# One planner attribute for the "own term" copies, and a new order of all engines, in an RWKV-6 + channel-MLP kernel

## The chip, the cores and the metric

The kernel runs on one core of a Trainium2 chip. The metric is the device time of the whole launch in microseconds, as a median over runs; lower is better.

## What is computed

An RWKV-6 attention block feeds a channel MLP with a residual. Everything is float32; B = 4, H = 8, S = 768, D = 48, so the model width is H*D = 384.

```python
# attention: r, k, v, w (B, H, S, D), u (H, D)
for t in range(S):
    cur = einsum('bhd,bhe->bhde', u[None] * k[:, :, t], v[:, :, t])
    y[:, :, t] = einsum('bhd,bhde->bhe', r[:, :, t], state + cur)
    state = w[:, :, t, :, None] * state + einsum('bhd,bhe->bhde', k[:, :, t], v[:, :, t])
x = y.transpose(0, 2, 1, 3).reshape(B, S, H * D)
# MLP
xn = (x - mean) / sqrt(var + 1e-6) * g_ln
out = x + maximum(xn @ w_ch1, 0) @ w_ch2        # w_ch1 (384, 1536), w_ch2 (1536, 384)
```

## The kernel before

**Tiling.** The work is cut into eight rounds (4 batches x 2 halves of 384 steps). A round has three tiles of 128 steps; each tile is cut into chunks of 64 steps, and a chunk into groups of four steps (Q = 4). Round 0 is done in two parts, its first tile alone (part c0 = 0) and its other two tiles (c0 = 1), so that the first products can start early.

**Front of a round.** `load` fetches w, k and r (`nat_w`, `nat_k`, `nat_r`). `inner` forms the products inside a group of four steps (`pad_k`, `pad_r`, `rk`, and again `nat_k`, `nat_r`, `nat_w`), and reductions write the sums to `vals`. These sums, the "own terms" (a step with itself and with the steps of its own group), go to DRAM (`own_d`) and come back in another layout as `va`. `place_own` then copies them into the diagonal of the matrix `A` with a predicated copy: data `va`, mask `mask_own`, both in SBUF. There are 18 such copies, all on DVE. `turn` transposes `pad_k` and `pad_r` on PE (`k_ps`, `r_ps`) and ACT copies them out; `turn_w` does the same for the decays (`w_ps`). For four levels, `quads` multiplies r by k on PE in many small matmuls (`a<-r,k`), `grow` scales k and r on DVE by the decays `tot` (`k<-k,tot`), and `keep` copies a level's result from PSUM into `A` (DVE: `A<-mask,a`). `states` makes and scans the states (`a<-v,k` on PE, `s<-s,decay,a` on DVE). `inside` multiplies `A` by v (`a<-v,A`, `a<-vx,A`), `outputs` adds the states' part (`a<-s,r`).

**Back of a round.** `normalize` (`stats`, `mv`, `rstd`, `xn`), transposes (`xT_ps`), and the MLP. Round 0 multiplies by the weights directly (`h_ps<-xf,w`); from round 1 on, x and the weights are cut in high, low and difference parts (`xhl`, `xd`; `wh`, `wl`, `w1diff`), and a round's first product starts with `h_ps<-xd,d`. `convert` turns the loaded weights into floats (`raw`, `held`, `w<-w`, `w<-w,held`, `ffn`).

**What sets the order.** Each step is handed to `Plan.add` with its engine (or a choice of engines), a cost, what it reads and writes, and the buffers that it takes. A table, `ORDER`, then lists every step once: the entry modulo 10000 is the step, the thousands choose among the engines that it may run on. `Plan.order` walks through that table, keeps a clock for each engine by the costs, and from it decides three things: which home (SBUF slot or PSUM bank) a buffer gets, how many filler matmuls (`idle`) go in front of a PE step that is planned to wait for more than 0.35 us, and which DVE steps a GpSimd step has to wait for. Each engine then runs its steps in the order of the table.

**The shared port.** `Plan.add` takes `port`, true for steps that may run on GpSimd and for those that say so. Such steps are planned one after the other on DVE and GpSimd:

```python
if op.port and e in held:
    t = max(t, held["POOL" if e == "DVE" else "DVE"])
...
if op.port and e in held:
    held[e] = t + cost
```

A filler is put in only where a PSUM bank of kind `b` is free by the plan at that time:

```python
home = min(self.homes[idle[0]], default=None)
if n and home and home[0] <= free["PE"]:
    out.append(lambda n=n, home=home: idle[2](n, home[1]))
```

## Time and profile before

| | before |
|---|---|
| median of 3 runs | 469.9 us (469.14 to 469.95) |
| span of the profiled execution, first to last instruction | 466.7 us |
| median less span | 3.2 us |
| PE busy | 458.0 us (98% of the span), 7442 records |
| DVE busy | 353.2 us (76%), 742 instructions |
| ACT busy | 263.8 us (57%), 608 instructions |
| GpSimd (POOL) busy | 137.7 us (30%), 141 instructions |

The execution that was profiled has no time of its own beside its span; a time is worked out here as a change of that span, set against the median. All instructions go through one helper, so they carry one line (L47) and are told apart by the names of their tiles, `out<-in`. A busy PE is not a PE that does useful work: fillers count as busy, and the ends of matmuls are modelled. Each float32 matmul of the fillers and of the small products leaves two records in the trace.

### The profile page before, as it was taken

Reading aid. Unit: us, or ns where it says so; the run is one execution under the profiler, and the core shown is the slowest. Engines: PE = TensorE matmul, PEld = TensorE weight load, DVE = VectorE, ACT = ScalarE, POOL = GpSimd, SP = SyncE. Lnnn points to the kernel's source line nnn. Section 1 sums busy time; section 2 is a strip of 40 time slices with the busy share of each in tenths; the row PEclk is TensorE's granted clock in tenths of the full one; section 3 lists DMA queues with packets and bytes.
Section 4 is the critical chain, followed back from the end, with each engine's and each line's share of the span. In section 5 each row is a group of like instructions: output and inputs, shape, how many; then the busy total and the mean of one; then the engine's idle time right before and its main releaser. Section 6 shows DMA issues by size and latency. Waiting matters only on the chain.

```text
span 466.7 us, 17460 instructions
## 1 busy us (share of the span) xinstructions
PE 458.0 (98%) x7442; PEld 399.7 (86%) x7442; DVE 353.2 (76%) x742; ACT 263.8 (57%) x608; POOL 137.7 (30%) x141
## 2 busy tenths in 40 slices
PE   8999999999999999999999999999999999999996
PEld 5677989766999666989776899999999999999996
DVE  8999999999997768897879887976733535525535
ACT  4697889754765322665621677855555456444440
POOL 4137013332451242353443240221013122321030
PEclk9999999999999999999999999999999999999999
DMA  7987775776658505745630545302222232142011
GB/s 208 277 199 210 205 156 137 233 196 156 174 150 185 111 28 136 166 138 145 157 61 5 86 124 129 111 30 70 84 62 67 76 103 67 37 136 67 35 51 51
DMA packets 105501, 56.23 MB, mean 120 GB/s; under 512 B 61904, under 2 KB 102352, under 8 KB 105424
## 3 DMA queue, kind: packets, MB, share of 16 engines
q1 hardware_dynamic: 105152, 54.92, 45.1%
q8 instruction: 58, 0.95, 0.9%
q10 hardware_dynamic: 272, 0.20, 0.1%
q14 instruction: 19, 0.16, 0.1%
HBM read 45.27 MB, written 7.47 MB: 113 GB/s over the span
## 4 chain that ended last, share of the span: by engine, by line
PE 84%; DVE 10%; POOL 2%; issue 2%; SPq 1%; DMA 1%; DVEq 0%; POOLq 0%
PE h_ps L47 28%; PE a L47 26%; PE o L47 15%; PE o_2P L47 4%; PE o_2D L47 2%; PE k_ps L47 2%; PE r_ps L47 2%; PE kn_ps L47 2%; PE xT_ps L47 2%; DVE nat_k L47 1%; DVE s L47 1%; DVE A L47 1%; SPq L47 1%; DVE vals L47 1%; DMA nat_k<-in_k_dram 1%
## 5 line engine op out<-in xcount | busy, mean ns | idle before, releaser
L47 ACT ACTIVATE h<-h_ps 128x384 f32<-128x384 f32 (+2 forms) x108 | 47.8, 456 | 49.6 <-PE h_ps L47 48.9
L47 PE MATMUL o<-ffn,h 128*128 128x384 f32 x216 | 74.7, 492 | 0.0
L47 DVE SCALAR_TENSOR_TENSOR hD<-hH,hL 128x384 fp32r<-128x384 f32 x60 | 36.3, 616 | 37.1 <-POOL hL L47 16.0
L47 POOL TENSOR_TENSOR hL<-h,hH 128x384 fp32r<-128x384 f32 x28 | 30.1, 1081 | 102.7 <-PE a L47 27.7
L47 ACT ACTIVATE h_ps<-h_ps 128x384 f32<-128x384 f32 x84 | 39.7, 481 | 34.5 <-PE h_ps L47 33.5
L47 PEld LDWEIGHTS o<-ffn,h 128*128 128x128 f32 x216 | 39.2, 190 | 23.1
L47 PEld LDWEIGHTS a<-r,k 48*56 48x56 f32 (+3 forms) x3072 | 39.7, 122 | 10.5 <-issue 4.9
L47 PE MATMUL h_ps<-xd,d 128*128 128x384 f32 x204 | 47.1, 335 | 0.0
L47 PE MATMUL a<-r,k 48*56 48x32 f32 (+3 forms) x3072 | 44.1, 208 | 0.6 <-issue 0.2
L47 PE MATMUL h_ps<-xhl,wl 128*128 128x384 f32 x180 | 40.4, 334 | 0.0
L47 DVE TENSOR_TENSOR r<-r,tot 112x768 f32<-112x768 f32 (+1 forms) x40 | 32.2, 808 | 10.0 <-PE a L47 10.0
L47 PE MATMUL h_ps<-xhl,wh 128*128 128x384 f32 x180 | 39.1, 326 | 0.0
L47 ACT ACTIVATE hH<-h 128x384 fp32r<-128x384 f32 x60 | 29.7, 518 | 11.6 <-PE a L47 7.8
L47 DVE TENSOR_TENSOR k<-k,tot 112x768 f32<-112x768 f32 (+1 forms) x40 | 31.6, 790 | 5.5 <-PE a L47 5.4
L47 PEld LDWEIGHTS h_ps<-xd,d 128*128 128x128 f32 x204 | 34.0, 189 | 0.5
L47 DVE TENSOR_TENSOR hL<-h,hH 128x384 fp32r<-128x384 f32 x32 | 17.9, 568 | 20.0 <-PE a L47 9.5
L47 PEld LDWEIGHTS h_ps<-xhl,wh 128*128 128x128 f32 x180 | 30.8, 189 | 0.0
L47 ACT COPY A<-a 32x384 f32<-32x384 f32 (+5 forms) x56 | 23.5, 421 | 12.4 <-PE a L47 9.8
L47 PEld LDWEIGHTS h_ps<-xhl,wl 128*128 128x128 f32 x180 | 30.1, 189 | 0.2
L47 PE MATMUL a<-w2D,hD 128*128 128x384 f32 x90 | 29.7, 330 | 0.4 <-DVE hD L47 0.4
L47 PE MATMUL idle<-nought 128*128 128x384 f32 (+2 forms) x90 | 27.9, 431 | 0.9 <-DVE eps L47 0.9
L47 ACT ACTIVATE xf<-xT_ps,g_sb 128x384 f32<-128x384 f32 (+2 forms) x27 | 14.7, 549 | 22.1 <-PE xT_ps L47 18.9
(184 smaller groups left out, 1135.3 us busy)
## 6 DMA issues: line engine op xcount, KB each, us to landing
d<-w1d SPq DMA_DIRECT2D x84, 192.0 KB, 2.6
raw<-in_moe_w_ch_dram SPq DMA_DIRECT2D x24, 384.0 KB, 4.0
nat_r<-in_r_dram SPq DMA_DIRECT2D x24, 192.0 KB, 3.8
nat_w<-in_w_dram SPq DMA_DIRECT2D x24, 192.0 KB, 4.1
v<-in_v_dram SPq DMA_DIRECT2D x24, 192.0 KB, 4.2
nat_k<-in_k_dram SPq DMA_DIRECT2D x23, 192.0 KB, 3.9
out_dram<-x SPq DMA_DIRECT2D x15, 192.0 KB, 2.0
w1d<-w1diff SPq DMA_DIRECT2D x12, 192.0 KB, 2.9
```

The source lines that it names most:

```text
L47: ins = self.tc.keep_in_program_order(f(*args, **kw))
```

## The change

`place_own` hands its copies to the planner with `port=True`; before, these copies had no such mark, so that GpSimd's steps could be planned beside them. The mark itself gives no instruction. The table `ORDER` is another one: the steps stand in the order of their planned start times, and the order on every engine is new, as is the choice of engine for some steps. Fillers, homes of buffers and the DVE steps that GpSimd waits for follow from it. No step is added or taken away.

```diff
@@ class Plan @@
     ORDER = [
-        10008, 3, 4, 10012, 2, 9, 10, 5, 11, 16, 264, 261, 7, 14, 13, 18, 10019, 262, 17, 265, 260, 263,
...
+        2, 3, 4, 5, 260, 262, 263, 261, 12, 10, 14, 265, 9, 13, 8, 15, 264, 16, 25, 11, 110, 17, 65, 18, 26,
...
     ]
@@ place_own @@
             plan.add(
                 "DVE", cost(part, 0.155, 0.98), lambda j=j: place(j),
                 r=[(va, i, c0) for i in ((0,), (1, 2))[j]] + [(A_, "nought")] + after,
-                w=[(A_, 0, c0, j)], pri=urgent(part, 10),
+                w=[(A_, 0, c0, j)], pri=urgent(part, 10), port=True,
             )
```

In all, the program before has 45 filler matmuls on PE with 12,288 columns, the changed one 34 with 9,344; all of them stand ahead of PE's first products `h_ps<-xf,w`. Some steps change engines: among them four products `nat_k<-nat_k,nat_r` of a whole round leave GpSimd, which keeps none, for DVE; three squarings `nat_w<-nat_w` go the other way; ACT takes over both clearings of `A` and four more copies `x<-a`.

Three places are shown.

First DVE, up to the second pair of own-term copies of round 0 (part c0 = 1; `mask_own`). Before:

```order
L47 TENSOR_TENSOR nat_k<-nat_k,u_bc 128x1152
L47 COPY_PREDICATED A_83<-mask_own,va_374 128x4x64
L47 COPY s_647<-a_67 112x48 x2
L47 SCALAR_TENSOR_TENSOR s_647<-s_647,decay_201,a_67 112x48 x2
L47 COPY s_668<-a_66 112x48 x2
L47 SCALAR_TENSOR_TENSOR s_668<-s_668,decay_201,a_66 112x48 x2
L47 TENSOR_REDUCE vals_75<-nat_k 128x3x2x4
L47 COPY_PREDICATED A_83<-mask_own,va_374 128x2x4x64
L47 TENSOR_REDUCE vals_75<-nat_r 128x6x2x2
L47 COPY_PREDICATED A_83<-mask_own,va_374 128x2x4x64
L47 SCALAR_TENSOR_TENSOR s_647<-s_647,decay_201,a_67 112x48 x6
L47 SCALAR_TENSOR_TENSOR last_767<-s_647,decay_201,a_67 112x48 x2
```

And DVE at the same place now:

```order
L47 TENSOR_REDUCE vals_75<-nat_k 128x3x2x4
L47 BN_STATS stats_705<-x_667 128x6
L47 TENSOR_REDUCE vals_75<-rk_0_565 128x3x2x2
L47 BN_AGGR mv_706<-stats_705 128x2
L47 SCALAR_TENSOR_TENSOR s_585<-s_585,decay_176,a_67 112x48 x6
L47 SCALAR_TENSOR_TENSOR last_732<-s_585,decay_176,a_67 112x48 x2
L47 SCALAR_TENSOR_TENSOR s_607<-s_607,decay_176,a_66 112x48 x6
L47 SCALAR_TENSOR_TENSOR last_753<-s_607,decay_176,a_66 112x48 x2
L47 TENSOR_REDUCE vals_75<-nat_r 128x6x2x2
L47 COPY_PREDICATED A_83<-mask_own,va_302 128x2x4x64 x2
L47 TENSOR_SCALAR w_3_1_114<-w_3_1_114 128x384
L47 TENSOR_SCALAR w_3_2_115<-w_3_2_115 128x384
```

The pair of copies now stands together, behind the sixteen scan steps (`s`, `last`) and the first `stats`, which stood behind it before. Up to and with the second copy of the pair, DVE runs 93 instructions before and 107 now.

Then PE between the second `inside` of round 0 (`a<-v,A`, c0 = 1) and the first products, `h_ps<-xf,w`. Before, behind that `inside`:

```order
L47 MATMUL idle<-nought 128x128
L47 MATMUL a_67<-s_668,r_210 64x48 x16
L47 MATMUL r_ps_2_879<-ident,pad_r 112x128 x4
L47 MATMUL idle<-nought 128x128
L47 MATMUL xT_ps_2_0_898<-ident,xn_0_891 128x128
L47 MATMUL w_ps_0_903<-ident,w_73 112x128 x3
L47 MATMUL k_ps_1_907<-ident,pad_k 112x128 x4
L47 MATMUL xT_ps_0_0_919<-ident,xn_0_891 128x128
L47 MATMUL xT_ps_1_0_921<-ident,xn_0_891 128x128
L47 MATMUL a_66<-s_647,r_210 64x48 x16
L47 MATMUL idle<-nought 128x128
L47 MATMUL a_67<-r_802,k_872 60x32 x48
```

And now, ahead of that `inside` (it begins right behind the last row; no filler stands after it, and the first products follow on its `a<-s,r` and `w_ps`):

```order
L47 MATMUL xT_ps_0_0_750<-ident,xn_0_741 128x128
L47 MATMUL idle<-nought 128x384
L47 MATMUL k_ps_0_767<-ident,pad_k 112x128 x4
L47 MATMUL xT_ps_2_0_776<-ident,xn_0_741 128x128
L47 MATMUL k_ps_2_780<-ident,pad_k 112x128 x4
L47 MATMUL k_ps_1_786<-ident,pad_k 112x128 x4
L47 MATMUL r_ps_0_795<-ident,pad_r 112x128 x4
L47 MATMUL r_ps_2_803<-ident,pad_r 112x128 x4
L47 MATMUL r_ps_1_809<-ident,pad_r 112x128 x4
L47 MATMUL xT_ps_1_0_817<-ident,xn_0_741 128x128
```

All transposes of round 1 (`k_ps`, `r_ps`) and of the first normalized tile (`xT_ps`) have moved ahead of `inside`, and the three fillers behind it are gone; one product `a<-r,k` of 48 matmuls that stood ahead of the first products now stands behind nine of them.

Last the start of PE. Before:

```order
L47 MATMUL idle<-nought 128x384 x7
L47 MATMUL idle<-nought 128x128
L47 MATMUL k_ps_0_182<-ident,pad_k 112x128 x4
L47 MATMUL idle<-nought 128x384
L47 MATMUL idle<-nought 128x128
L47 MATMUL r_ps_0_191<-ident,pad_r 112x128 x4
L47 MATMUL w_ps_0_196<-ident,w_73 112x128
```

And now:

```order
L47 MATMUL idle<-nought 128x384 x3
L47 MATMUL idle<-nought 128x128
L47 MATMUL w_ps_0_166<-ident,w_73 112x128
L47 MATMUL idle<-nought 128x384 x3
L47 MATMUL idle<-nought 128x256
L47 MATMUL r_ps_0_190<-ident,pad_r 112x128 x4
L47 MATMUL idle<-nought 128x128
L47 MATMUL k_ps_0_203<-ident,pad_k 112x128 x4
```

The small transpose `w_ps` comes first, in the middle of the long stretch of fillers, and the fillers between the transposes are fewer.

## The prediction

> **What bounds the kernel now.** I read the page first: its busy line and the line of the chain.

> ```profile
> span 466.7 us, 17460 instructions
> PE 458.0 (98%) x7442; PEld 399.7 (86%) x7442; DVE 353.2 (76%) x742; ACT 263.8 (57%) x608; POOL 137.7 (30%) x141
> ...
> PE 84%; DVE 10%; POOL 2%; issue 2%; SPq 1%; DMA 1%; DVEq 0%; POOLq 0%
> ```

> PE is busy for 98% of the span, so a new order can win only what PE does for nothing: waits, and fillers, which count as busy. Next the view by windows, to see in which stage which engine is full (columns: length, then busy us and records of PE, weight loads, DVE, ACT, POOL; granted clock; DMA share; GB/s).

> ```profile
> 0.00:20.00 20.00, 17.48 (x155) 11.56 (x157) 18.16 (x44) 11.37 (x21) 5.99 (x18) 1.00 0.82 239
> 20.00:40.00 20.00, 19.76 (x444) 14.07 (x437) 19.85 (x49) 16.27 (x42) 9.86 (x8) 1.00 0.85 205
> 40.00:60.00 20.00, 19.36 (x549) 17.66 (x551) 19.21 (x50) 17.37 (x48) 6.20 (x8) 1.00 0.67 198
> 60.00:140.00 80.00, 80.00 (x1502) 64.83 (x1495) 78.00 (x161) 56.90 (x134) 27.25 (x24) 1.00 0.68 175
> 140.00:310.00 170.00, 169.01 (x3886) 140.19 (x3885) 140.07 (x295) 87.11 (x196) 55.26 (x54) 1.00 0.46 110
> 310.00:460.00 150.00, 150.00 (x930) 149.24 (x929) 74.42 (x142) 74.80 (x169) 33.19 (x31) 1.00 0.23 68
> ```

> From 310 us on PE is full and DVE half empty: nothing to win there. From 140 to 310 PE lacks 1.0 us, and DVE has 30 us to spare. Up to 140 us both look full, and DVE lacks only 4.8 us in all. The first stretch is where PE's fullness is false. The groups by line and form show the fillers (busy time, mean ns of one record; every filler leaves two):

> ```profile
> L47 PE MATMUL idle<-nought 128*128 128x384 f32 x44 | 18.7, 543 | 0.9 <-DVE eps L47 0.9
> L47 PE MATMUL idle<-nought 128*128 128x128 f32 x32 | 6.6, 287 | 0.0
> L47 PE MATMUL idle<-nought 128*128 128x256 f32 x14 | 4.6, 409 | 0.0
> ```

> That makes 22, 16 and 7 fillers, 29.9 us by these rows (a little less in truth, since neighbours overlap): six per cent of the kernel in which PE waits for the front of round 0. It waits there mainly for DVE, which runs 57.2 of the first 60 us. So two bounds follow each other: DVE until the first products can run freely, then PE. A gain must come from the first 50 us, and must survive until DVE has room at 140 us.

> **Part one, the fillers.** The changed program has 17, 12 and 5 fillers. At 18.7/22 = 0.85, 6.6/16 = 0.41 and 4.6/7 = 0.66 us each that is 14.5 + 4.9 + 3.3 = 22.7 us, 7.2 less than 29.9. But a filler only pictures a planned wait. Where no PSUM bank is free by the plan, none is put in, and PE simply waits. So -7.2 us is the favourable end of this term; the other end is 0, if every removed filler becomes a bare wait.

> **Part two, what DVE allows.** The second `inside` of round 0 needs the second pair of own-term copies. The timeline of DVE there:

> ```profile
> 38.48 1.13 DVE L47 COPY_PREDICATED A<-mask_own,va 128x512 f32<-128x512 int8 x1
> 39.50 1.34 DVE L47 TENSOR_REDUCE vals<-nat_r 128x24 f32<-128x1152 f32 x1
> 40.76 0.76 DVE L47 COPY_PREDICATED A<-mask_own,va 128x512 f32<-128x512 int8 x1
> 41.38 1.14 DVE L47 SCALAR_TENSOR_TENSOR s<-s,decay,a 112x48 f32<-112x48 f32 x6
> 42.42 0.45 DVE L47 SCALAR_TENSOR_TENSOR last<-s,decay,a 112x48 f32<-112x48 f32 x2
> ```

> The pair ends at 40.76 + 0.76 = 41.52. In the new order sixteen scan steps come first: (42.42 - 41.38)/6 = 0.173 each, +2.8 us. Of the other steps that cross this point two more leave than enter (107 against 93 instructions up to here, sixteen of them the scan). Their sizes run from 0.76 to 1.34 us by the neighbours above; I take the two at the lower end of that, -1.5 in all, with 0 and -2.7 as bounds. Two copies of one size took 1.13 and 0.76: the longer one had GpSimd work beside it, and the new plan keeps such steps apart, -0.4 (bounds 0 and -0.4). The pair then ends at 41.52 + 2.8 - 1.5 - 0.4 = 42.4.

> PE before, at the same place:

> ```profile
> 42.82 0.65 PE L47 MATMUL k_ps<-ident,pad_k 128*112 128x128 f32 x4 [0.64 <-POOL pad_k L47]
> 43.31 0.60 PE L47 MATMUL r_ps<-ident,pad_r 128*112 128x128 f32 x4
> 43.74 0.60 PE L47 MATMUL k_ps<-ident,pad_k 128*112 128x128 f32 x4
> 44.27 0.25 PE L47 MATMUL a<-v,A 64*64 64x48 f32 x1
> ...
> 45.35 0.49 PE L47 MATMUL idle<-nought 128*128 128x128 f32 x2
> ...
> 46.87 0.39 PE L47 MATMUL idle<-nought 128*128 128x128 f32 x2
> ...
> 48.89 0.49 PE L47 MATMUL idle<-nought 128*128 128x128 f32 x2
> ...
> 50.81 0.94 PE L47 MATMUL h_ps<-xf,w 128*128 128x128 f32 x6
> ```

> `inside` starts at 44.27; it would start at 42.5, -1.8. By then PE has done more: one group each of `k_ps` and `r_ps` (43.74 - 43.31 = 0.43 each) and three `xT_ps` (a quarter of that each, 0.3), so another -1.2. Three fillers behind it go, 0.49 + 0.39 + 0.49 with their tails, -1.1 net. Sum at the first products: -4.1 us, against -7.2 by the fillers. The difference is bare waiting, which I expect right ahead of `inside`: nine transposes run there with four banks of that kind.

> **Part three, whether it holds.** The next place where DVE is short is the first split product of round 1:

> ```profile
> 118.36 0.55 DVE L47 SCALAR_TENSOR_TENSOR xd<-xhl 128x384 fp32r<-128x384 f32 x1
> ...
> 118.99 0.73 PE L47 MATMUL h_ps<-xd,d 128*128 128x384 f32 x3
> ```

> The third `xd` ends at 118.91, and PE starts on it 0.08 us later: no slack. Up to that `xd` the new order has 256 DVE instructions, before 257, so DVE gives nothing here; but ahead of this product PE will have done more (from the order): 12 more `kn_ps`, 4 `r_ps`, 24 `a<-v,k` and 12 pairs of `a<-v,A` and `a<-vx,A`.

> ```profile
> L47 PE MATMUL kn_ps<-ident,k 112*128 112x112 f32 x96 | 13.7, 263 | 0.0
> L47 PE MATMUL a<-v,A 64*64 64x48 f32 x384 | 14.1, 220 | 0.4 <-DVE last L47 0.3
> L47 PE MATMUL a<-v,k 64*48 64x48 f32 x768 | 11.8, 207 | 0.0
> ```

> By busy time per matmul of the program: 12 x 13.7/96 = 1.7, 4 x 0.43/4 = 0.4, 24 x 11.8/384 = 0.7, 12 x 14.1/192 = 0.9, together 3.7. These shares hold each group's tail; without it I put it at 2.9 (four fifths). With DVE 0.4 us earlier, as above, the gain at 119 us is 3.3. It is the smaller of the two sums, so it counts: -3.3 us.

> **Part four, the port.** The copies' mark speaks of a collision that the trace shows later:

> ```profile
> 197.30 2.09 DVE L47 COPY_PREDICATED A<-mask_own,va 128x768 f32<-128x768 int8 x1
> ...
> 199.54 3.01 POOL L47 TENSOR_TENSOR nat_k<-nat_k,nat_r 128x1152 f32<-128x1152 f32 x1 [1.03 <-DVE A L47]
> ...
> 207.55 0.65 PE L47 MATMUL h_ps<-xd,d 128*128 128x384 f32 x3
> ...
> 208.47 0.25 PE L47 MATMUL a<-v,A 64*64 64x48 f32 x1 [0.26 <-DVE last L47]
> ```

> This copy took 2.09 us beside GpSimd work. The chain of waits runs from it through `nat_k` on GpSimd, and PE pays where `a<-v,A` follows at 208.47, after 0.26 us idle. The long `nat_k` steps leave GpSimd altogether. I take -0.4, between this 0.26 and the 1.0 that PE lacks in all from 140 to 310 us; bounds 0 and -1.0. [...]

> The tail behind PE's last matmul is six DVE sums and a store as before: 0. Total: -3.3 - 0.4 = -3.7 us. The span goes from 466.7 to 463.0, and the median, 3.2 us above the span, from 469.9 to **466.2 us**.

> **Rivals.** (a) The fillers are true: DVE is less held up than I count, and the whole -7.2 of part one comes, with 0.4 of the port: 462.3. For it: four long products leave GpSimd, and DVE loses 4.8 us in the first 140 to waits. Against it: the exact hand-over at 118.9.

> (b) The waits eat it: DVE in the new order is held as long as now, with the bound of 0 for the two steps and the transposes ahead of `inside` held by ACT; each filler becomes a bare wait, and the time stays at 469 to 470.

> (c) Slower, by GpSimd being locked out:

> ```profile
> 30.72 5.37 POOL L47 TENSOR_TENSOR decay<-tot 112x8 f32<-112x8 f32 x1 [9.36 <-DVE pad_k L47]
> ```

> This step of eight columns took 5.37 us, while DVE ran without a gap; it hurt nobody, since its reader came later on DVE. In the new order GpSimd keeps more of the steps that lie between loads and transposes (`nat_w`, `pad_r`). If one that PE's transposes await is locked out so, about 5 us are lost less a slack of under 1. From the second such hold on (2 x 4.3 = 8.6 against 3.7) the kernel is slower: 469.9 + 4.9 = 474.8. Against it: a POOL total of 30%, and fewer steps there.

> (d) The clock. The first fillers are slow: the tile's records have a median of 483 ns and, at the start alone, up to 1007 ns:

> ```profile
> L47 PE MATMUL idle<-nought x90: 272/483/1007, 0.9 to 49.1; 128*128 128x384 f32 x44, 128*128 128x128 f32 x32, 128*128 128x256 f32 x14
> ```

> Bare waits in place of fillers could bring that back: some three large matmuls at twice the time, 3 x 0.5 = 1.5 us for each relapse, 467.7 with one. The granted clock stood at 1.00 in all windows with waits of 0.64. [...]

> **How the numbers follow.** Forecast of a part of the fillers' gain, with (d) in it: 0.50. (a) or better: 0.20. (b): 0.14. (c): 0.16. The likeliest is 466.2; its own range is 464 to 468.5. The range of 8 in 10 goes from 461.5, just past (a), to 470.5, past (b), and leaves out (c) and little else. About 0.2% (0.9 us) can be told from no change. Faster by more than that: 0.47 of the first, all of (a), 0.03 of (b), 0.70. Within it: 0.03 + 0.10 = 0.13. Slower: (c) and the rest of (b), 0.17.

> **What would show it.** Right: first products `h_ps<-xf,w` start near 46.7 us (50.81 - 4.1), with some 48 `a<-r,k` not yet done; an idle PE of one to three us ahead of the second `inside`; `h_ps<-xd,d` at 118 to 119 with more done before it; no own-term copy of a round far over 1.1 us. Wrong: `xd` waiting on GpSimd, a GpSimd step of 3 us or more that PE awaits, a granted clock under 1.00 at 40 to 50 us, or more idle PE from 140 to 310 us than the 1.0 now.

## The result, and the profile after

The changed kernel takes 466.8 us (median of 20 runs, 464.2 to 471.5), the kernel before beside it 469.6 us. The ratio is 0.9941, with a 95% interval of 0.9918 to 0.9965: 0.6% faster, where 466.2 us and 0.8% had been forecast. Medians and ranges here are of all runs, ratios of the fast ones alone (within 1.5% of the fastest of their kernel). The profiled execution has a span of 464.0 us, 2.7 less than before; 463.0 had been forecast. (Its time is 465.8 us, 1.8 above the span, as in every run on record; 466.7 + 1.8 = 468.5 us, so the profiled execution before was quicker than its kernel's median.)

The page of the changed kernel, the busy line and the line of the chain:

```profile
span 464.0 us, 17396 instructions
PE 452.5 (98%) x7420; PEld 396.1 (85%) x7420; DVE 354.9 (76%) x747; ACT 271.3 (58%) x622; POOL 102.8 (22%) x125
...
PE 87%; DMA 4%; ACT 3%; DVE 3%; issue 1%; SPq 1%; POOL 0%; DVEq 0%; ACTq 0%
```

PE is as full as before, on a span that is shorter. On the chain DVE has gone from 10% to 3%, and DMA (1% before) and ACT have come in: in this execution PE's front hangs on weights that ACT converts. The windows, cut as before:

```profile
0.00:20.00 20.00, 16.99 (x220) 11.82 (x221) 17.11 (x49) 14.19 (x25) 5.16 (x16) 1.00 0.84 234
20.00:40.00 20.00, 17.73 (x422) 12.86 (x421) 18.77 (x52) 17.03 (x45) 7.60 (x11) 1.00 0.77 187
40.00:60.00 20.00, 19.52 (x510) 17.24 (x509) 18.99 (x46) 18.33 (x49) 2.47 (x5) 1.00 0.76 221
60.00:140.00 80.00, 80.00 (x1487) 64.20 (x1486) 78.98 (x160) 56.06 (x130) 19.91 (x21) 1.00 0.66 166
140.00:310.00 170.00, 169.60 (x3889) 142.73 (x3881) 144.65 (x302) 93.69 (x215) 37.78 (x46) 1.00 0.50 116
310.00:460.00 150.00, 148.64 (x917) 147.20 (x915) 75.82 (x144) 72.03 (x163) 29.88 (x28) 1.00 0.22 66
```

Up to 40 us PE is idle for 5.3 us, before for 2.8: bare waits have come where fillers were. From 140 to 310 us it lacks 0.4 us, before 1.0. The fillers, by groups and forms:

```profile
L47 PE MATMUL idle<-nought 128*128 128x384 f32 x34 | 14.6, 548 | 1.2 <-DVE eps L47 0.9 <-issue 0.3
L47 PE MATMUL idle<-nought 128*128 128x128 f32 x24 | 4.9, 287 | 0.0
L47 PE MATMUL idle<-nought 128*128 128x256 f32 x10 | 3.4, 422 | 0.0
```

Their busy time fell from 29.9 to 22.9 us, the 7 us of the prediction's part one. How much of that became time gained is read from PE's records. I priced every matmul by the mean interval from its start to the start of the next matmul (by its kind: names and shape, over both traces, without the waits), and compared the work that PE has behind it at the same time. The lead of the changed kernel, in us:

| at | first products | 62 us | 140 | 220 | 260 | 312 | 420 | 450 | end of PE | span |
|---|---|---|---|---|---|---|---|---|---|---|
| lead | 3.2 | 2.7 | 2.5 | 2.3 | 2.7 | 4.3 | 4.2 | 3.3 | 3.3 | 2.7 |

Four pieces: 2.7 us are won up to 62 us, stay about the same to 260, 1.6 more come to 312, and 1.5 are lost again behind 420. The same ledger by kinds, over the whole span: the work itself is the same in both (each kind at its shortest usual interval, 378.8 us). Above it stand the pieces of this table, before and after. A tiled matmul here is one on at most 64 rows of PE's array (`a<-r,k`, `a<-v,k`, `a<-v,A`, `a<-s,r`); a plain one fills 112 or 128.

| us | fillers | single waits over 0.15 | changes between tiled and plain matmuls | small rest | after PE's last matmul |
|---|---|---|---|---|---|
| before | 28.8 | 2.1 | 11.2 | 40.6 | 4.3 |
| after | 24.2 | 4.7 | 10.1 | 40.4 | 4.8 |

(A filler counts here to the start of the next matmul, with the wait behind it.) Of the differences, -4.6 + 2.6 - 1.1 - 0.2 + 0.6 = -2.7 us, the first two belong to the front.

### The profile page after: what moved, and what is told of

Its sections match the earlier page's. It is cut to its first block, busy times and chain, and to the rows that moved or that the text cites. A ratio compares the mean times of both kernels' runs of the same rounds, so it can differ in the third digit from the quotient of the medians.

```text
span 464.0 us, 17396 instructions
## 1 busy us (share of the span) xinstructions
PE 452.5 (98%) x7420; PEld 396.1 (85%) x7420; DVE 354.9 (76%) x747; ACT 271.3 (58%) x622; POOL 102.8 (22%) x125
## 4 chain that ended last, share of the span: by engine, by line
PE 87%; DMA 4%; ACT 3%; DVE 3%; issue 1%; SPq 1%; POOL 0%; DVEq 0%; ACTq 0%
PE h_ps L47 31%; PE a L47 26%; PE o L47 15%; PE o_2P L47 4%; DMA raw<-in_moe_w_ch_dram 3%; PE o_2D L47 2%; PE k_ps L47 2%; PE kn_ps L47 2%; PE xT_ps L47 2%; PE r_ps L47 2%; ACT held L47 1%; SPq L47 1%; DMA nat_k<-in_k_dram 1%; DVE x L47 1%; DVE nat_k L47 1%
## 5 line engine op out<-in xcount | busy, mean ns | idle before, releaser
L47 ACT ACTIVATE h<-h_ps 128x384 f32<-128x384 f32 (+2 forms) x108 | 47.7, 455 | 63.1 <-PE h_ps L47 60.6
L47 PE MATMUL o<-ffn,h 128*128 128x384 f32 x216 | 75.2, 490 | 0.0
L47 DVE SCALAR_TENSOR_TENSOR hD<-hH,hL 128x384 fp32r<-128x384 f32 x60 | 36.0, 615 | 46.4 <-POOL hL L47 31.9
L47 ACT ACTIVATE h_ps<-h_ps 128x384 f32<-128x384 f32 x84 | 39.7, 478 | 40.0 <-PE h_ps L47 39.3
L47 PEld LDWEIGHTS o<-ffn,h 128*128 128x128 f32 x216 | 38.9, 191 | 21.1
L47 POOL TENSOR_TENSOR hL<-h,hH 128x384 fp32r<-128x384 f32 x26 | 27.1, 1049 | 117.0 <-ACT hH L47 39.9
L47 PEld LDWEIGHTS a<-r,k 48*60 48x60 f32 (+3 forms) x3072 | 39.5, 122 | 10.9 <-issue 3.8
L47 PE MATMUL h_ps<-xd,d 128*128 128x384 f32 x204 | 46.6, 336 | 0.0
L47 PE MATMUL a<-r,k 48*60 48x32 f32 (+3 forms) x3072 | 43.5, 208 | 1.1 <-issue 0.4
L47 PE MATMUL h_ps<-xhl,wl 128*128 128x384 f32 x180 | 40.9, 336 | 0.0
L47 PE MATMUL h_ps<-xhl,wh 128*128 128x384 f32 x180 | 39.1, 327 | 0.0
L47 DVE TENSOR_TENSOR r<-r,tot 112x768 f32<-112x768 f32 (+1 forms) x40 | 31.6, 795 | 6.7 <-PE a L47 5.7
L47 PEld LDWEIGHTS h_ps<-xd,d 128*128 128x128 f32 x204 | 34.5, 190 | 1.4 <-ACT tot L47 0.3
L47 DVE TENSOR_TENSOR k<-k,tot 112x768 f32<-112x768 f32 (+1 forms) x40 | 31.8, 801 | 3.8 <-PE a L47 3.8
L47 ACT ACTIVATE hH<-h 128x384 fp32r<-128x384 f32 x60 | 30.1, 522 | 5.2 <-PE a L47 3.9
L47 DVE TENSOR_TENSOR hL<-h,hH 128x384 fp32r<-128x384 f32 x34 | 19.5, 577 | 15.3 <-ACT hH L47 9.5
L47 PEld LDWEIGHTS h_ps<-xhl,wh 128*128 128x128 f32 x180 | 30.9, 190 | 0.0
L47 PE MATMUL a<-w2D,hD 128*128 128x384 f32 x90 | 30.2, 336 | 0.5 <-DVE hD L47 0.5
L47 PEld LDWEIGHTS h_ps<-xhl,wl 128*128 128x128 f32 x180 | 29.9, 190 | 0.5
L47 ACT COPY A<-a 32x384 f32<-32x384 f32 (+5 forms) x60 | 25.3, 424 | 7.2 <-PE a L47 5.5
L47 PE MATMUL a<-w2L,hL 128*128 128x384 f32 x80 | 26.1, 327 | 0.0
L47 PE MATMUL a<-w2H,hH 128*128 128x384 f32 x80 | 26.1, 327 | 0.0
```

What stands on the lines that cost most here:

```text
L47: ins = self.tc.keep_in_program_order(f(*args, **kw))
```

## The experiments

Each kernel was timed beside the kernel before on the same chip; ratios are against that one. The three groups ran on three chips, where the kernel before took 468.9, 469.3 and 469.4 us, so numbers are compared inside a group. First group: the changed kernel again, and three kernels with more DVE work.

**The changed kernel, again.** No edit.

> The changed kernel itself, once more. In its first trace PE ends 4.84 us before the span's end (before the change 4.28), and PE stands still 0.51 us at 444.77 for an hD. Theory (the order is fixed, so its waits are): span 462.5 to 466, the wait for hD at about 444 us is there again with 0.4 to 0.6 us. Rival (chance of one execution): that wait is gone or stands elsewhere. If the 0.56 us more behind PE's last matmul belong to the store's landing and not to the order, this stretch comes out anywhere from 4.2 to 4.9.

466.1 us (12 runs), ratio 0.9936 (0.9913 to 0.9960), span 464.3. Rows of PE, this execution:

```profile
22.02 0.49 PE L47 MATMUL idle<-nought 128*128 128x128 f32 x2 [1.13 <-issue]
...
47.24 1.95 PE L47 MATMUL h_ps<-xf,w 128*128 128x128 f32 x16
...
445.04 0.43 PE L47 MATMUL a<-w2D,hD 128*128 128x384 f32 x1 [0.50 <-DVE hD L47]
```

The late wait for an hD is there again, and 4.83 us lie behind PE's last matmul. In all the kernels with the new table this last stretch is 4.82 to 4.84 us; with the old table it is 4.28, 4.33, 4.34 and, resorted, 4.60. So both losses of the end are the order's, not one execution's. What differs is the front: here PE stood still for 1.13 us with no releaser ("issue"), and the first products came 1.1 us later than in the first trace.

**Own-term copies twice.** One edit each for round 0 (its second pair), round 2 and round 4:

```diff
-            DVE.copy_predicated(out=to, data=v_, mask=m)
+            for _ in range(2 if rnd == 2 else 1):
+                DVE.copy_predicated(out=to, data=v_, mask=m)
```

> The changed kernel with the second pair of own-term copies of round 0 made twice (the same values): DVE has 2 x 0.73 = 1.46 us more at 42 us, nothing else changes. Theory (DVE sets the front up to the first products, and PE is full from 62 us on, so that what is lost early stays lost): second inside and first products 1.0 to 1.5 us later, time +1.0 to +1.5 us against the changed kernel run beside it. Rival (PE, ACT or the fillers set the front): under +0.4 us.

468.3 us, 2.1 above the changed kernel beside it. Its rows, and one window of 2 us (the column behind POOL's is the granted clock):

```profile
41.10 2.91 DVE L47 COPY_PREDICATED A<-mask_own,va 128x512 f32<-128x512 int8 x4
...
44.07 0.25 PE L47 MATMUL a<-vx,A 64*64 64x48 f32 x1 [1.07 <-DVE A L47]
...
47.78 1.49 PE L47 MATMUL h_ps<-xf,w 128*128 128x128 f32 x10
```

```profile
46.00:48.00 2.00, 2.00 (x48) 1.91 (x44) 2.00 (x7) 1.56 (x5) 0.00 (x0) 0.50 1.02 380
```

PE waits 1.07 us more for the copies, and right behind it the clock is at 0.50. The first products start at 47.8 us; in six executions whose front is that of the changed kernel they start at 45.1 to 47.2 (mean 45.8). So DVE sets the front, as the theory has it: PE's wait names its copy. The first products come 2.0 later than that mean and the median is 2.1 higher, the clock included, but the 2.1 us of scatter among the six leave the size open.

> The changed kernel with both own-term copies of round 2 made twice: DVE has 2 x 1.02 = 2.04 us more at 103 to 110 us. In the changed kernel the third xd of round 1 ends at 118.84 us and PE starts on it at 119.18. Prediction's step (DVE without slack at this hand-over binds the time): the product starts 2.04 - 0.34 = 1.7 us late, time +1.0 to +1.7 us. Rival (PE is full by itself from 62 to 140 us, DVE has some slack that the trace shows as waits in it, 1.0 us in the 80 us): between 0 and +0.7 us.

470.1 us, 4.0 more: both expectations were too low. Rows of DVE and PE of the profiled execution (its span is 4.6 above that of the changed kernel run again), and the line of queue 8, whose packets the profile calls "instruction", here from 214 to 223 us and in the changed kernel from 212 to 221:

```profile
112.48 0.62 PE L47 MATMUL k_ps<-ident,pad_k 128*112 128x128 f32 x4 [1.15 <-DVE pad_k L47]
...
119.38 1.02 DVE L47 SCALAR_TENSOR_TENSOR xd<-xhl 128x384 fp32r<-128x384 f32 x2
...
120.45 1.24 PE L47 MATMUL h_ps<-xd,d 128*128 128x384 f32 x6
...
221.52 0.23 PE L47 MATMUL a<-r,k 48*48 48x32 f32 x2 [2.12 <-issue]
```

```profile
q8 instruction: 1, 0.02, 0.7%
```

```profile
q8 instruction: 2, 0.03, 2.0%
```

In this execution PE's lead falls from 3.3 us at 62 to 1.2 at 140, the whole 2.04 us. The largest part of it is lost ahead of the hand-over: at 112.48 PE has waited 1.15 us for the `pad_k` that DVE makes right behind the second doubled copy. At the hand-over PE then starts on the product 0.05 us after the third xd. DVE has no slack in this stretch, as the prediction's part three said, but it binds PE at `pad_k` first. Another 2.12 us are a hole at 219 to 221 us with no releaser: by the trace's DMA records a packet of 16 KB on queue 8 began at 209.99 us and the next at 219.01, in the changed kernel at 208.44, 214.06 and 218.30. One execution's hole doesn't explain the median of twelve; the executions sorted by clock, below, say more of it.

> The changed kernel with both own-term copies of round 4 made twice: DVE has 2 x 1.02 = 2.04 us more past 140 us, where it is idle for 3.2 us of 140 to 180 and 9.4 us of 180 to 220. Theory (PE alone bounds there): time within 0.4 us of the changed kernel, PE's first products unmoved. Rival (DVE paces the whole kernel): +1 to +2 us.

467.5 us as a median, 1.4 above the changed kernel, which by itself would speak for the rival. But four of the twelve executions have a mean clock of 0.986 to 0.994, and the median of the other eight is 466.0 (466.1 in the changed kernel run again, the same way). The profiled execution has a span of 462.3, the shortest of this group. Its lead grows from 3.5 us at 140 to 6.0 at 312, by 2.5, in the kernel run again by 2.3: nothing was lost to the two copies. Behind 140 us DVE doesn't pace PE.

Second group, one step each.

**The late low parts on DVE.** The MLP's hidden values h are cut in high, low and difference parts, `hH`, `hL` and `hD`. The table's last twelve `hL` on GpSimd get DVE:

```diff
-        11830, 11836, 11942, ..., 12126, 12132, 12138, 12150
+        1830, 1836, 1942, ..., 2126, 2132, 2138, 2150
```

> The changed kernel with its twelve last low parts hL on DVE instead of GpSimd, at the same places of the order. In both traces of the changed kernel PE loses 1.0 us past 312 us, 0.67 + 0.10 of it at 444 us ahead of an hD, whose hL took GpSimd 0.99 us (on DVE one takes 0.55). Theory (GpSimd's length makes these two waits): the loss past 312 us falls from 1.0 to 0.3 us or less; time -0.7 to -1.0 us. Rival (the chain through ACT and hD is late anyway): 0.5 us or more stays.

What it mends in the changed kernel (rows of GpSimd, of PE and of DVE's last sum; the second DVE row is the kernel before's last sum):

```profile
442.33 1.97 POOL L47 TENSOR_TENSOR hL<-h,hH 128x384 fp32r<-128x384 f32 x2 [8.53 <-ACT hH L47]
...
444.77 0.43 PE L47 MATMUL a<-w2D,hD 128*128 128x384 f32 x1 [0.51 <-DVE hD L47]
...
460.08 0.62 DVE L47 SCALAR_TENSOR_TENSOR x<-o_2P,rstd,x 128x384 f32<-128x384 f32 x1
```

```profile
463.16 0.62 DVE L47 SCALAR_TENSOR_TENSOR x<-a,rstd,x 128x384 f32<-128x384 f32 x1
```

With the edit no row of PE past 380 us shows idle time, and single waits past 312 us fall from 1.0 to 0.2 us: the theory holds in the trace. The time (468.1 us, ratio 0.9948, 0.9915 to 0.9980) doesn't show it: seven of the twelve executions have a mean clock of 0.996 or less, with 468 to 473 us, and five have 464.0 to 465.8. The front is that of the changed kernel, so these falls can hardly be the edit's.

**Twelve more switches.** At twelve places of the table a plain product moves in front of the last tiled step ahead of it, for example:

```diff
-        ..., 546, ..., 683, ...
+        ..., 683, 546, ...
```

> The changed kernel with twelve plain products (h_ps and the like) moved in front of the last small tiled product before them, at twelve places from 70 to 300 us: 24 more changes between tiled and plain matmuls, the same work. In the traces such a change costs 0.094 us into tiled and 0.136 us out of it, above the same matmul without one. Theory (the new order gains 1.1 us because it has fewer of them): 12 x 0.23 = 2.8 us slower. Rival (the price only shows where PE would wait anyway): under 1 us.

471.7 us, ratio 1.0073 (1.0047 to 1.0098). Past 60 us the trace has 51 changes each way instead of 39, at the same medians, 0.094 us into tiled and 0.136 out: 12 x 0.23 = 2.8 us. PE's lead over the kernel before goes from 3.5 us at 62 to -0.9 at 312, by 6.0 us more than in the changed kernel: 2.8 the switches, 1.6 one hole with no releaser at 220 us, and 1.6 that were not traced further. The price of a switch is real; the whole change was more than that price.

**No fillers.**

```diff
-    for fn in plan.order(busy, ("b", 0.24, idle)):
+    for fn in plan.order(busy):
```

> The changed kernel without its 34 filler matmuls. The prediction took fillers as pictures of waits; the busy time of all of them is 22.9 us. Theory (they fill waits): first products within 1 us of the 45.1 to 47.2 us seen so far, time within 1 us. Rival (d) (they keep the clock up): real matmuls of the first 60 us take up to twice their time, 8.9 us of work before the first inside, of which most lies in waits; 1 to 5 us slower. Third (they hold PE up): 1 to 3 us faster.

485.4 us as the median of its six executions (477.5 to 489.7), 16 above the kernel before beside it (469.3), far beyond the worst that I expected. The groups up to 60 us, of this kernel and of the changed one run again:

```profile
L47 PE MATMUL k_ps<-ident,pad_k 128*112 128x128 f32 x24 | 6.0, 423 | 1.2 <-POOL pad_k L47 0.8 <-DVE pad_k L47 0.5
```

```profile
L47 PE MATMUL k_ps<-ident,pad_k 128*112 128x128 f32 x24 | 3.3, 275 | 0.7 <-ACT r L47 0.4 <-POOL pad_k L47 0.3
```

The same transposes take 423 ns instead of 275. Two equal transposes show when that ends:

```profile
42.85 0.42 PE L47 MATMUL xT_ps<-ident,xn 128*128 128x128 f32 x1
...
47.29 0.27 PE L47 MATMUL xT_ps<-ident,xn 128*128 128x128 f32 x1
```

The first clock record of this trace stands at 47.2 us. In the other thirteen it stands at 3.8 to 6.9 us, and in the twelve of them with fillers of 384 columns such a filler takes 0.85 us ahead of it and 0.49 behind. By these times PE starts at a low clock; with the fillers it is up within 7 us, without them only at 47.2, behind most of the front. (The windows print 1.00 where no record stands, so they hide this.) The first products come at 49.9 us, 4 late. Another 8 us go from 220 to 312 us: PE stands still with no releaser for 2.0 us at 229 and 1.7 at 268, and behind each the clock falls, for example (268 us):

```profile
266.00:270.00 4.00, 2.34 (x166) 2.19 (x154) 1.43 (x2) 1.41 (x3) 0.00 (x0) 0.89 0.06 18
270.00:274.00 4.00, 4.00 (x32) 3.26 (x29) 2.40 (x4) 1.33 (x3) 0.00 (x0) 0.50 0.02 4
```

Fillers aren't only pictures of waits: in the front they bring the clock up, which is rival (d) of the prediction, priced far too low. Why such holes come behind 220 us without them was not tried.

**Conversions moved back.** Nine conversions of loaded weights stand two or three steps later on ACT, for example:

```diff
-        ..., 111, 43, 112, ...
+        ..., 43, 112, ..., 111, ...
```

> The changed kernel with nine conversions of loaded weights (held and w out of raw) moved later on ACT by two or three of its steps, up to 56 us, behind steps that wait for no load. In its first trace ACT waited 3.4 us for such loads, and the first products came at 46.1 us; where ACT hardly waited (0.5 us, with round 4's copies twice) they came at 45.1. Executions of the changed kernel spread from 463.4 to 471.5 us, those of the kernel before from 468 to 472. Theory (ACT standing in order behind late loads makes part of this spread): ACT's wait for raw under 0.5 us, first products at 45 to 46 us, median 0.5 to 1.5 us lower. Rival (the spread comes from how PE is supplied with instructions, 2.5 us of idle PE with no releaser in the second trace against 0.3 in the first): median and spread as before, 466 +- 1.

467.5 us, ratio 0.9975 (0.9947 to 1.0004). ACT's wait for loaded weights (3.1 us ahead of `held` in the first trace) is gone, but it was gone in the changed kernel run again too, whose first products came at 47.2 us. The profiled execution here is one of the long ones (span 469.7), and it shows what this one lost. A row of PE, and the windows of 2 us (the column behind POOL's is the granted clock):

```profile
21.87 1.66 PE L47 MATMUL idle<-nought 128*128 128x384 f32 x4 [1.62 <-issue]
```

```profile
20.00:22.00 2.00, 0.38 (x2) 0.13 (x2) 1.99 (x6) 1.94 (x6) 0.45 (x2) 1.00 0.84 243
22.00:24.00 2.00, 2.00 (x28) 1.34 (x32) 0.00 (x0) 0.01 (x1) 0.00 (x0) 0.58 0.66 159
24.00:26.00 2.00, 2.00 (x85) 1.81 (x81) 1.20 (x4) 0.91 (x4) 0.00 (x0) 0.50 1.01 289
...
34.00:36.00 2.00, 2.00 (x34) 0.85 (x33) 0.60 (x5) 1.97 (x5) 1.10 (x1) 0.50 0.15 42
36.00:38.00 2.00, 1.97 (x41) 1.53 (x37) 2.00 (x6) 1.49 (x5) 0.18 (x2) 1.00 0.00 0
```

PE stands still with no releaser for 1.62 us, and then the clock is 0.50 for 14 us, although PE is busy all the time. The first products come at 51.2 us instead of 45 to 47. The theory on ACT falls; the rival, which counts PE's idle time with no releaser, stands for this execution.

Third group: parts of the change alone, and fuller fillers.

**The mark alone**, on the old table.

```diff
-                w=[(A_, 0, c0, j)], pri=urgent(part, 10),
+                w=[(A_, 0, c0, j)], pri=urgent(part, 10), port=True,
```

> The kernel before with port=True on the own-term copies and its old table: only fillers (14,592 columns for 12,288), homes and a few names follow from the mark, the order on each engine stays. Theory (the mark by itself brings nothing; the new table brings the whole gain): within 1 us of the kernel before. Rival (the mark's planning helps by itself, or the 2,304 columns more, some 5 us of PE by 18.7/22 us for one of 384, hold PE up): 2 us or more to either side.

472.7 us, ratio 1.0073 (1.0047 to 1.0099): slower. Its fillers, and its first products:

```profile
L47 PE MATMUL idle<-nought 128*128 128x384 f32 x56 | 23.1, 538 | 0.9 <-DVE eps L47 0.9
...
53.97 2.27 PE L47 MATMUL h_ps<-xf,w 128*128 128x128 f32 x18
```

The planner now expects longer waits and puts in fillers that hold PE up: the first products come 3.2 us later than before, at the same work. In the new table the mark changes nothing: without it that program has the same instructions on every engine. So the whole gain is the table's, and the new attribute itself does nothing in it.

**The old entries, sorted by planned start**, each engine's order kept (example: the table begins with 3, 4, 5 where it began with 10008, 3, 4).

> The kernel before with its own entries merely sorted by their planned start: each engine keeps its order, but homes, banks and the DVE steps that GpSimd awaits are decided in the new sequence (fillers 12,032 columns for 12,288). Theory (handing in by planned times alone changes next to nothing): within 1 us of the kernel before. Rival (it is the sequence of the table, not the order of the engines, that gains): -2 to -3 us.

470.4 us, ratio 1.0016 (0.9992 to 1.0040): no gain. Handing in by planned times alone brings nothing; the new order on the engines does.

**Fewer fillers in the kernel before.**

```diff
-    for fn in plan.order(busy, ("b", 0.24, idle)):
+    for fn in plan.order(busy, ("b", 0.28, idle)):
```

> The kernel before with a filler unit of 0.28 in place of 0.24 us: 9,344 columns of fillers, as many as the changed kernel has, 24% fewer than before. Theory (fewer fillers leave the clock without margin): one or more of twelve executions at a mean clock under 0.99 and over 472 us, as 4 of 32 of the changed kernel were, while none of 35 of the kernel before was under 0.996. Rival (the falls need the 1 to 2 us in which PE got no instructions, which came with the new order's denser start): spread as before, 468 to 472 us, clock 0.996 or more.

470.6 us, ratio 1.0009 (0.9984 to 1.0034). Six of twelve executions have a mean clock of 0.990 to 0.996; of the kernel before beside it four of 35 have 0.996 or less, the lowest 0.988; of the one with the mark, which has the most fillers, none of twelve is under 0.998. None passed the line that I had drawn (under 0.99 and over 472 us; no execution of the changed kernel had passed it either, three of 32 were under 0.99), so neither side is shown: it leans to the theory. The rival's premise doesn't hold as I put it: this trace has the old order and a hole of 1.09 us with no releaser at 27.6 us.

**Fuller fillers, and the late hL on DVE.**

```diff
-            now = min(n, TT)
+            now = min(n, 4)
...
-    for fn in plan.order(busy, ("b", 0.24, idle)):
+    for fn in plan.order(busy, ("b", 0.2, idle)):
```

> The changed kernel with the twelve late hL on DVE, a filler unit of 0.20 us (10,752 columns for 9,344) and fillers of up to 512 columns for 384 (so fewer instructions). Theory (falls of the clock make the upper part of the changed kernel's spread, and fuller fillers keep it up): no execution under a clock of 0.99, median 464.5 to 466, 0.8 of it by the late hL. Rival (the falls come from the supply of instructions, which no filler mends): two or more of twelve above 469.5 us with a clock under 0.995, median 466 to 468.

468.4 us as the median of all twelve, 1.0 below the kernel before beside it; ratio 0.9940 (0.9907 to 0.9973). The profiled execution has a span of 462.4 us and its first products at 45.1, but five of twelve are at a clock of 0.983 to 0.992, with 469 to 474 us. The rival is borne out in its times: fuller fillers don't keep the clock from falling. That the falls come from the supply of instructions is not shown by this run. No version here beats the changed kernel with certainty.

**The executions sorted by clock.** The falls of the clock hide effects of 1 us, and the traces show how to set them apart. Where no stretch at 0.50 is recorded before PE's end, an execution's mean clock is 0.997 to 1.000 (eleven traces); with one, three and four such stretches of 3.41 us it is 0.995, 0.989 and 0.985. I read a mean of 0.996 or less as at least one fall. The medians of the executions without one, sorted after the fact:

| kernel | without a fall | their median | the kernel before beside it |
|---|---|---|---|
| changed, run again | 11 of 12 | 466.1 | 468.9 |
| round 0 twice | 7 of 12 | 467.4 | 468.9 |
| round 2 twice | 7 of 12 | 468.3 | 468.9 |
| round 4 twice | 8 of 12 | 466.0 | 468.9 |
| late hL on DVE | 5 of 12 | 464.9 | 469.3 |
| conversions moved back | 6 of 12 | 466.9 | 469.3 |
| fuller fillers, late hL on DVE | 4 of 12 | 464.9 | 469.3 |

Read so, the copies of round 0 cost 1.3 us, as the theory had it, those of round 2 cost 2.2 and those of round 4 nothing. The late hL gain: 4.4 us below the kernel before, where the changed kernel is 2.8 below in its own group. The numbers of executions are small. How often the clock falls also differs between groups with the same front (five of 32 executions of the changed kernel, seven of twelve with the late hL), and why is open.

## Why the prediction was right, step by step

**The shape was right, the sum in part by luck.** Fillers fell by 7.0 us of busy time (forecast 7.2), and part of them became bare waits. But the total of 3.7 is nearer to the measured 2.7 to 2.8 than its terms are: part three was 0.7 too large, 1.2 to 1.4 us that stood in no term came between 140 and 312 us, and 1.5 us that stood in no term were lost at the end. That the last two cancel is luck. The rows of the changed kernel at the places of parts two and three:

```profile
36.26 0.57 PE L47 MATMUL a<-v,k 64*48 64x48 f32 x32 [1.12 <-ACT k L47]
...
42.08 1.35 DVE L47 COPY_PREDICATED A<-mask_own,va 128x512 f32<-128x512 int8 x2
...
43.03 0.31 PE L47 MATMUL a<-v,A 64*64 64x48 f32 x2
43.48 0.25 PE L47 MATMUL a<-vx,A 64*64 64x48 f32 x1
...
46.13 2.17 PE L47 MATMUL h_ps<-xf,w 128*128 128x128 f32 x18
48.24 1.57 PE L47 MATMUL a<-r,k 48*60 48x32 f32 x96
```

**Part two.** The pair of copies ends at 43.43 us (forecast 42.4), `inside` starts at 43.03 (42.5), though all but its first two records start at 43.48, right behind the pair, and the first products at 46.13 (46.7), with 48 `a<-r,k` not yet done, as foreseen. At equal work that is a lead of 3.2 us, where I had summed 4.1. The start at 46.7 was near by luck: the sum of 4.1 holds no term for those 48 `a<-r,k` (1.57 us), and with them it gives 45.2.

The step that missed is the pair's end, put 1.0 too early. From `inside` on the terms hold: without the 48 `a<-r,k` the way to the first products is 2.4 us shorter (forecast 1.2 + 1.1). Up to the end of the pair DVE's work was to grow by 0.9 us (2.8 - 1.5 - 0.4). It is the same as before, but DVE's waits grow by 2.1 us, from 2.0 to 4.1, and the sum put them at nothing. The busy time of DVE up to the pair's end, before and after:

```profile
0.00:41.52 41.52, 39.53 (x94) 1.00 0.83 226
```

```profile
0.00:43.43 43.43, 39.31 (x108) 1.00 0.78 203
```

It waits for loads (`pad_k` for `nat_k` 1.2 us, for `nat_w` 0.7), for products of the states (0.6) and for ACT (0.4). This part scatters: in four other executions of this front the pair ends at 42.4 to 42.5 and the first products start at 45.1 to 45.2, as the terms give it, and in the changed kernel run again it ends at 44.5. The largest bare wait of PE is not ahead of `inside` but at 36.26, for ACT.

**Part three** named the right place for a wrong moment:

```profile
117.83 1.01 DVE L47 SCALAR_TENSOR_TENSOR xd<-xhl 128x384 fp32r<-128x384 f32 x2
...
119.18 1.24 PE L47 MATMUL h_ps<-xd,d 128*128 128x384 f32 x6
```

The third xd ends at 118.84, nearly as before (118.91), but PE comes 0.34 us after it: in this execution PE, not DVE, is the later one. The lead of 2.6 us had been fixed by 62 us, and simply lasts. The term of 3.3 was 0.7 too large. The 2.9 us of work counted ahead of this product are 2.8 at mean intervals (the traces show nine more `kn_ps` there, where I had counted 12); the step that failed is the 0.4 us that DVE was to bring, since PE comes 0.2 us later than before instead. That DVE is the next bound near there is what the copies of round 2, made twice, showed, at `pad_k` 8 us ahead of the product.

**Part four** had its own term right, and more came besides: 0.4 forecast, 1.6 to 1.8 us came between 140 and 312. The copies of a whole round, before and after:

```profile
L47 DVE COPY_PREDICATED A<-mask_own,va 128x768 f32<-128x768 int8 x14 | 15.5, 1104 | 0.0
```

```profile
L47 DVE COPY_PREDICATED A<-mask_own,va 128x768 f32<-128x768 int8 x14 | 14.1, 1028 | 0.0
```

The longest copy of a round takes 1.08 us, before 2.09; the wait of 0.26 us at 208 us is gone, and from 204 to 212 us the lead grows by 0.4 us (0.4 to 0.5 in the seven other traces with the new table that I compared). The copy of 2.09 us had an `rk` of GpSimd beside it (197.09 to 198.50 us). The copies at 122.93 and 227.39 us before took 1.04 and 1.02, but the `pad_k` on GpSimd beside them 2.53 and 2.97 us, where 18 of the 24 GpSimd steps of its shape take 1.41 to 1.46. PE's idle time from 140 to 310 us falls from 1.0 to 0.4 us in all, inside the bounds, but only the 0.26 of it are the wait of part four; the largest other wait that is gone is one of 0.43 us for an hD at 305.8. The rest was no term of the sum: past 60 us the new order has 39 changes into tiled matmuls for 42, and 39 out of them for 43, which is 3 x 0.094 + 4 x 0.136 = 0.8 us. Idle time (0.6) and switches are 1.4; the last 0.2 to 0.4 are spread thin.

**The end** was put at 0 and cost 1.5 us: 0.9 by GpSimd's hL (1.01 us each in the median, on DVE 0.55) on the way to two hD, 0.6 behind PE's last matmul. The forecast looked at the number of DVE's last sums, which is the same. The last two of them end 1.5 us after PE, before 1.4; the other 0.4 us lie behind DVE's last sum, and what makes them is open.

**The rivals.** (a), the whole 7.2, was reached by no median; the best executions of the changed kernel, 463.4 us, came near it. (b) is half of what happened to the fillers. (c) did not come. (d) came in five of 32 executions of the changed kernel (mean clock 0.983 to 0.995, 470.1 to 471.5 us), with a price of some 4 us against the 466 of the others, not 1.5. In the traces the falls come behind stretches of 3.41 us in which PE was busy to 0.42 to 0.63, not idle, and over the executions they took less than the order gained.

## What to carry to other kernels

Compare two orders at equal work, not at equal time: a front's gain shows early and then only lasts, and what is lost at the end shows apart. Fillers on a waiting PE are real work: with too many they delay it (+3 us here), without them the clock comes up 40 us later (+4 us at the first products) and falls again behind holes. Here PE also stood still with no releaser for up to 2.12 us at a time; look at "issue" and at the instruction queue before tightening a front further. Sort executions by their mean clock before comparing effects of 1 us.

## What the runs showed of the hardware

**PE's long holes with no releaser end behind a packet of one DMA queue.** The holes of PE named "issue" told above, of 1.13 to 2.12 us, are the long ones of 31 over 0.25 us, in twelve of the fourteen traces, three of these traces of kernels with the old entries. By the DMA records each of the 31 ends 1.10 to 1.61 us after a packet of 16 KB on queue 8 has ended. And each stands at the same place of a packet: a trace has 58 such packets for some 14,840 matmuls and weight loads, 256 each, and the number of records that PE has begun ahead of a hole, semaphore ones counted with them, (450, 706, 961 and so on) is always 193 or 194 above a multiple of 256. I read this as PE waiting for that packet; no record names it as what PE waits for. The first packet begins at 16.4 to 18.0 us in seven executions with the new table and no hole over 1 us in the front, and at 19.5 in both that have one (at 20.2 without fillers, where the front has none). DMA was at 0.84 in the quoted window of the hole of 1.62 us and at 0.06 in that of the hole at 268 us; what makes a packet late is open.

```profile
41.37:44.78 3.41, 2.14 (x58) 1.50 (x59) 3.34 (x8) 2.91 (x7) 0.00 (x0) 1.00 0.95 280
```

```profile
18.92:22.33 3.41, 1.79 (x41) 1.00 (x33) 3.07 (x9) 3.00 (x9) 0.45 (x2) 1.00 0.85 251
```

```profile
217.28:220.69 3.41, 2.12 (x101) 1.82 (x101) 1.73 (x4) 1.55 (x4) 0.27 (x1) 1.00 0.81 217
```

What brings the clock back is open: in the 14 us at 0.50, PE's records fill every piece.

**A change between tiled and plain matmuls** costs 0.094 us in and 0.136 us out of it, the same within 0.002 us in all fourteen traces.
